# Step i+1's h on TensorE between step i's attention and its y, in a kernel of attention and two MoE layers

## The chip, the cores and the metric

The kernel runs on one core of a Trainium2 chip. The metric is the device time of one execution in microseconds; times of several runs are given by their median.

## The reference

Three layers in fp32. Retention-like attention on q, k, v of shape (4, 8, 576, 64); a dense MoE with 2304 tokens, 512 model and 2048 inner columns; a second MoE in which each of eight experts takes its 288 tokens in order of their gate values.

```python
scores = scale * np.matmul(q, k.transpose(0, 1, 3, 2))
ret = scores * Dmat[None]                  # decay gamma**(i-j), 0 above the diagonal
x = np.matmul(ret, v)                      # -> (2304, 512)
h = x @ w_in                               # first MoE
g = h * np.tanh(np.log1p(np.exp(h)))       # (h > 20: h itself)
x = g @ w_out
logits = x @ w_gate                        # second MoE: greedy assignment, 288 tokens each
for e in range(8):
    out[mask_e] = np.maximum(x[mask_e] @ w1[e], 0) @ w2[e]
```

## The kernel before

fp32 operands are split into a high part and a rest (names ending in h and l), and each product is made of three matmul passes: high by high, rest by high, high by rest.

The attention and the first MoE run together, in one hand-written order (`first_part`). The tokens are cut into nine blocks of 256 (block n), the inner columns into 16 tiles of 128 (tile f). A **step** is one pair (n, f); there are 144. `plan` (line 65) mixes the steps of blocks 0, 1 and 2 in the first 48 steps, because the weights of each tile f are converted while they run; from step 48 on step i is block i // 16, tile i % 16.

A step's work, by function:

- `ff_h` (L309, matmuls at L317): 12 matmuls of TensorE make h (128 inner columns x 256 tokens) in PSUM. Two consecutive steps share a bank: an even step takes a new tile of one of the two tags ph0 and ph1, an odd step writes its second half.
- `ff_a1` (L321): ScalarE makes tanh (L326), square (L327) and a copy with scale (L328) into d; VectorE multiplies two halves (L334).
- `ff_a2`, `ff_b1`, `ff_b2`, `ff_b3`: VectorE's reciprocal (L339), the products with it (L344 on VectorE, or L346 and L347 on GpSimd), VectorE's product with h itself (L352), which reads the PSUM tile a last time, and the split into gh (ScalarE, L358) and gl (L359, on VectorE while weights are converted and on GpSimd later). In iteration i, b2 belongs to step i-1 and b3 to step i-2.
- `ff_y` (L397, matmuls at L411, for the last block `ff_y_last`, L439 and L447): six (or twelve half-sized) matmuls add g @ w_out of step i-3 into the block's two PSUM banks. After a block's last tile, ScalarE and VectorE copy y out (L420, L421).

Between these stand pieces that `slots` assigns to steps. An attention chunk (up to 128 tokens of a batch) has scores (L219 on TensorE, then pm on VectorE, L224), an output (L243, L248, then ScalarE's copy xh at L254 and VectorE's xl at L255) and a state (L273; then ScalarE, L285, for chunks 2 to 7, else VectorE, L281). The logit pieces of p_logits transpose y (L381; copies at L385 on ScalarE and L383 on VectorE) and multiply (L391). Pieces of the `idle` list (a grid for the later search, L630 to L643; logits on VectorE, L368) are taken near the end of an iteration.

Weights are converted by VectorE (L163, L168), ScalarE (L156, L159, L174) and GpSimd (L177), one part per iteration in nearly all of the first 30 iterations.

Each engine works through its own instructions in the order in which the loop emits them; semaphores follow from the tiles that instructions read and write, and PSUM is tracked by bank. The chunk outputs fall into steps 1, 3, 5, 6, 9, 40, 46, 57, 62, 67, 73, 82, 86, 91, 99, 105, 115 and 121; the logit pieces that turn y with ScalarE's copy into steps 48, 51, 56 and 131.

After the steps, `second_part` routes the tokens and runs the eight experts.

Of the kernel before, what the change touches and what calls it, by code (L numbers as in the profile page):

```python
# [64 lines left out]
def plan():  # L65


    spread = lambda a, b, n: [a + (b - a) * k // (n - 1) for k in range(n)]
    own = {i: (0, f) for f, i in enumerate([0, 1, 2, 3] + spread(6, ENDS[0], NF - 4))}
    free = [i for i in range(3 * NF) if i not in own]  # L70
    lead = [i for i in free if i < BEGIN2]
    rest = [i for i in free if BEGIN2 <= i]
    near = [i for i in rest if i <= ENDS[1]]
    ones = lead + [near[k] for k in spread(1, len(near) - 1, NF - len(lead))]
    own.update({i: (1, f) for f, i in enumerate(ones)})
    own.update({i: (2, f) for f, i in enumerate(i for i in free if i not in ones)})
    steps = [own[i] for i in range(3 * NF)]
    steps += [(n, f) for n in range(3, NB) for f in range(NF)]
    return steps


def first_part(ctx, tc, att, att_ht, att_hn, dtab, qtab, ktab, stab, wi, wo, wgb, ydram, L, constants, cst, begin, grid):
# [16 lines left out]
    steps = plan()  # L99
# [42 lines left out]
    class convert:  # L142
# [18 lines left out]
        def x(self):  # L161
            w0 = self.w0
            nc.vector.scalar_tensor_tensor(w0, self.w1, 0x80000000, w0, op0=ALU.bitwise_and,  # L163
                                           op1=ALU.bitwise_or)
# [16 lines left out]
    def x_block(n):  # L181
        if n not in xT:
            if n == 2:
                xT[n] = [sp.tile([P, KT, TB], F32R, tag="x2", name=f"x{k}2", bufs=2) for k in "hl"]
            else:
                xT[n] = [work.tile([P, KT, TB], F32R, tag="x" + k, name="x" + k, bufs=2) for k in "hl"]
        return xT[n]
# [121 lines left out]
    def ff_h(n, f, i):  # L309
        xh, xl = x_block(n)  # L310
        if i % 2 == 0:
            hbank[0] = psum.tile([P, 2, TB], F32, tag=("ph0", "ph1")[i // 2 % 2], name="ph")
        ph = hbank[0][:, i % 2, :]
        k = 0
        for kt in range(KT):
            for w, x in ((winh, xh), (winl, xh), (winh, xl)):
                nc.tensor.matmul(ph, w[f][:, kt, :], x[:, kt, :], start=(k == 0), stop=(k == 11))  # L317
                k += 1
        q2[n, f] = ph

    def ff_a1(n, f, i, alone):  # L321

        ph = q2[n, f]
        d = work.tile([P, 2, P], F32, tag="d", name="d", bufs=2)
        df = d.rearrange("p a b -> p (a b)")
        nc.scalar.activation(df, ph, AF.Tanh, scale=0.5)  # L326
        nc.scalar.activation(df, df, AF.Square, bias=half_b, scale=-0.5)  # L327
        nc.scalar.activation(df, df, AF.Copy, bias=0.5, scale=0.5)  # L328
        u = work.tile([P, 2, P], F32, tag="u", name="u", bufs=3)
        r = u[:, 0, :]  # L330
        if alone:

            r = work.tile([P, DM], BF, tag="scr", name="r").bitcast(F32)[:, :P]
        nc.vector.tensor_mul(r, d[:, 0, :], d[:, 1, :])  # L334
        inv[n, f] = (d, u, r, alone)

    def ff_a2(n, f):
        r = inv[n, f][2]
        nc.vector.reciprocal(r, r)  # L339

    def ff_b1(n, f, eng):
        d, u, r, alone = inv.pop((n, f))
        if alone:
            eng.tensor_mul(u, d[:, ::-1, :], r[:, None, :].to_broadcast([P, 2, P]))  # L344
        else:
            eng.tensor_mul(u[:, 1, :], d[:, 0, :], r)  # L346
            eng.tensor_mul(u[:, 0, :], d[:, 1, :], r)  # L347
        gt[n, f] = u.rearrange("p a b -> p (a b)")

    def ff_b2(n, f):  # L350
        g = gt[n, f]
        nc.vector.scalar_tensor_tensor(g, g, -1.0, q2.pop((n, f)), op0=ALU.add, op1=ALU.mult)  # L352

    def ff_b3(n, f, eng):
        g = gt[n, f]
        gh = work.tile([P, TB], F32R, tag="gh", name="gh", bufs=3)
        gl = work.tile([P, TB], F32R, tag="gl", name="gl", bufs=3)
        nc.scalar.activation(gh, g, AF.Copy)  # L358
        eng.tensor_sub(gl, g, gh.bitcast(F32))  # L359
        gt[n, f] = (gh, gl)  # L360
# [169 lines left out]
        x()  # L530
    for i in range(len(steps) + YL):
        new = i < len(steps)
        if i == 20:
            constants()
        if i == 62:
            stage.__exit__(None, None, None)
            late = tc.tile_pool(name="late", bufs=1)
            WG = late.__enter__().tile([P, E, DM], F32, name="WG")
            nc.sync.dma_start(WG, wgb)
        if now:  # L540
            now.x()
            now.a()
        if old:
            old.l()
        if new:
            n, f = steps[i]
            ff_h(n, f, i)
            for x in slots.get(i, []):
                x()
            ff_a1(n, f, i, bool(now or old))  # L550
        if new:

            eng = nc.vector if now or old else nc.gpsimd
            if i > 1:
                ff_b3(*steps[i - 2], eng)
            ff_a2(n, f)
            if i:
                ff_b2(*steps[i - 1])
            ff_b1(n, f, nc.vector if i == len(steps) - 1 else eng)
        if i == len(steps) - 1:  # L560
            ff_b2(n, f)
            ff_b3(*steps[i - 1], nc.gpsimd)
            ff_b3(n, f, nc.vector)
        if now:
            now.h()
        old, now = now, None
        if nxt and i in CONV:
            now, nxt = nxt, convert() if done[0] < len(parts) else None
            now.x1()
            now.c()  # L570
        for k in range(2 if i % 4 == 0 or TAIL <= i < POP2 else 1):
            if idle:
                idle.pop(0)()
        if late and i > TAIL + BEGIN and not idle:
            late = late.__exit__(None, None, None)
            soon.extend(begin())
        if i >= YL:
            ff_y(*steps[i - YL], i)
# [840 lines left out]
def build(tc, ap, out):  # L1419
    nc = tc.nc  # L1420
    with ExitStack() as ctx:
        pp = ctx.enter_context(tc.tile_pool(name="pp", bufs=1))
        dp = ctx.enter_context(tc.tile_pool(name="dp", bufs=1, space=bass.MemoryType.DRAM))
        cp = ctx.enter_context(tc.tile_pool(name="cp", bufs=1))
        ctx.enter_context(tc.manual_schedule())
        L = pp.tile([P, NT, E], F32, name="L")
        ydram = dp.tile([N, DM], F32, name="ydram")
        cst = {}
        start = []
        cs = ExitStack()  # L1430

        def begin():
            start.append(Search(cs, tc, L, cst))
            return start[0].early()

        with ExitStack() as c1:
            first_part(c1, tc, ap["att"], ap["att_ht"], ap["att_hn"], ap["dtab"], ap["qtab"],
                       ap["ktab"], ap["stab"], ap["wi"], ap["wo"], ap["wgb"], ydram, L, lambda: constants(cp, tc, ap, cst), cst, begin, lambda *a: Grid(cs, tc, L, cst).pieces(*a))
        keep = ctx.enter_context(tc.tile_pool(name="keep", bufs=1, reuse_waits="tile"))
        L0 = keep.tile([P, NT, E], F32, name="L0")  # L1440
        nc.gpsimd.tensor_copy(L0, L)
        with ExitStack() as c2:
            flag = second_part(c2, tc, L, ydram, ap["wx"], cst, out, start[0], True, L0)
            again = nc.values_load(flag[0:1, 0:1], min_val=0, max_val=1)
        cs.close()
        with tc.If(again != 0):
            with ExitStack() as c3:
                general_constants(c3, tc, ap, cst)
                second_part(c3, tc, L0, ydram, ap["wx"], cst, out, Start(c3, tc, L0, cst), False)
# [15 lines left out]
def constants(cp, tc, ap, cst):  # L1465
    nc = tc.nc
    load_constants(cp, tc, ap, cst, (("ident", [P, P], F32), ("J", [P, NJ + 1], F32), ("SCL", [P, 3], F32),
                                     ("pri", [P, E], F32), ("tri", [P, P], BF), ("io", [P, 96], BF),
                                     ("pcv", [P, NT, 2], BF), ("WGN", [P, KT, E], F32)))
    cst["ones"] = cp.tile([P, P], BF, name="c_ones")  # L1470
    nc.vector.memset(cst["ones"], 1.0)
# [69 lines left out]
```

## Time and profile before

| | us |
|---|---|
| median of 3 runs | 839.11 (837.38 to 840.23) |
| profiled execution | 837.55 |
| its span, first to last instruction | 835.5 |
| TensorE busy | 771.1 (92%) |
| VectorE busy | 546.5 (65%) |
| ScalarE busy | 437.5 (52%) |
| GpSimd busy | 475.3 (57%) |

The steps take the time from about 18 to about 536 us. The engine names in rows are PE (TensorE), DVE (VectorE), ACT (ScalarE) and POOL (GpSimd). A matmul's end is modelled, so neighbouring matmuls seem to overlap; starts are the safer numbers.

### The profile page before, as it was taken

What the parts mean: (1) busy time and instruction counts of PE and PEld (TensorE: products, weight loads), DVE (VectorE), ACT (ScalarE), POOL (GpSimd) and SP (SyncE); (2) the same over time, 40 slices, a digit from 0 to 9 for tenths busy, and PEclk for the clock granted to TensorE, in tenths of its full rate; (3) what the DMA queues carried; (4) which work ended last, traced back from release to release, by engine and by line L of the source; (5) the groups of instructions that cost most, each with busy time, mean ns of one, the idle gap of its engine ahead of it and who ended that gap; (6) DMA issues with size and microseconds to landing.
All of it is one profiled execution on the core that took longest, in us unless ns stands there. A gap on an engine that the chain in (4) does not pass through costs nothing.

```text
span 835.5 us, 16274 instructions
## 1 busy us (share of the span) xinstructions
PE 771.1 (92%) x6151; PEld 702.5 (84%) x6151; DVE 546.5 (65%) x1271; ACT 437.5 (52%) x963; POOL 475.3 (57%) x541
## 2 busy tenths in 40 slices
PE   6688888999999999999999999839999999999993
PEld 5577676888998888888888989839999999999992
DVE  4898999755555788897888875676656653442110
ACT  2678888645544445555455555323535553554520
POOL 2534333455545576666676655314877986977811
PEclk9999999999999999999999999959999999999997
DMA  8536344001212310310110000054566664655311
GB/s 317 192 121 218 133 136 145 2 26 51 102 49 104 114 35 5 101 52 29 51 49 27 2 26 2 26 170 146 153 182 187 195 186 150 200 157 173 119 30 32
DMA packets 27320, 87.63 MB, mean 105 GB/s; under 512 B 4448, under 2 KB 5600, under 8 KB 27104
## 3 DMA queue, kind: packets, MB, share of 16 engines
q1 hardware_dynamic: 24160, 77.06, 28.6%
q0 software_dynamic: 3072, 9.44, 3.5%
q8 instruction: 50, 0.82, 0.4%
q14 instruction: 38, 0.31, 0.1%
HBM read 77.05 MB, written 9.44 MB: 104 GB/s over the span
## 4 chain that ended last, share of the span: by engine, by line
PE 69%; DVE 15%; issue 7%; ACT 3%; POOL 3%; DMA 2%; SPq 0%; DVEq 0%; POOLq 0%; ACTq 0%
PE ph L317 20%; PE hp L1256 9%; PE op L1270 8%; PE b_E L411 8%; PE b_F L411 7%; DVE r L339 3%; DVE raw L163 2%; DVE u L344 2%; PE cnt L971 2%; PE b_A L219 2%; PE b_D L248 1%; DVE hot L867 1%; PE b_E L447 1%; DVE y L168 1%; POOL wxl L810 1%
## 5 line engine op out<-in xcount | busy, mean ns | idle before, releaser
L317 PE MATMUL ph<-xh,winh 128*128 128x256 f32 x576 | 164.6, 286 | 17.5 <-ACT d L326 13.0
L317 PE MATMUL ph<-xl,winh 128*128 128x256 f32 x576 | 161.5, 280 | 0.2 <-DVE xl L255 0.2
L317 PE MATMUL ph<-xh,winl 128*128 128x256 f32 x576 | 161.5, 280 | 0.0
L810 POOL TENSOR_TENSOR wxl<-wraw,wxh 128x1024 fp32r<-128x1024 f32 x60 | 142.3, 2396 | 29.4 <-ACT wxh L808 29.0
L359 POOL TENSOR_TENSOR gl<-u,gh 128x256 fp32r<-128x256 f32 x114 | 85.7, 752 | 89.4 <-ACT gh L358 88.6
L317 PEld LDWEIGHTS ph<-xh,winh 128*128 128x128 f32 x576 | 109.2, 190 | 31.9 <-ACT d L326 17.3
L326 ACT ACTIVATE d<-ph 128x256 f32<-128x256 f32 x144 | 54.7, 380 | 130.5 <-PE ph L317 115.0
L317 PEld LDWEIGHTS ph<-xh,winl 128*128 128x128 f32 x576 | 109.5, 190 | 4.4
L339 DVE RECIPROCAL u<-u 128x128 f32<-128x128 f32 x113 | 107.7, 953 | 3.9
L317 PEld LDWEIGHTS ph<-xl,winh 128*128 128x128 f32 x576 | 109.6, 190 | 0.4 <-DVE xl L255 0.4
L334 DVE TENSOR_TENSOR u<-d 128x128 f32<-128x128 f32 x113 | 44.7, 396 | 63.5 <-ACT d L328 54.9
L346 POOL TENSOR_TENSOR u<-d,u 128x128 f32<-128x128 f32 x112 | 52.4, 468 | 51.9 <-DVE u L339 51.8
L808 ACT ACTIVATE wxh<-wraw 128x1024 fp32r<-128x1024 f32 x64 | 67.4, 1053 | 17.4 <-DMA wraw<-in_wx_dram 17.4
L327 ACT ACTIVATE d<-d,half_b 128x256 f32<-128x256 f32 x144 | 73.5, 510 | 4.7
L347 POOL TENSOR_TENSOR u<-d,u 128x128 f32<-128x128 f32 x112 | 68.2, 609 | 8.8
L328 ACT ACTIVATE d<-d 128x256 f32<-128x256 f32 x144 | 60.2, 418 | 4.6
L358 ACT ACTIVATE gh<-u 128x256 fp32r<-128x256 f32 x144 | 57.9, 402 | 2.1 <-DVE u L352 2.0
L368 DVE SCALAR_TENSOR_TENSOR scr<-y,WG 128x512 bf16<-128x512 f32 x64 | 55.3, 863 | 0.4
L1247 DVE SCALAR_TENSOR_TENSOR htl<-hp,hth 128x288 fp32r<-128x288 f32 x64 | 28.4, 454 | 40.3 <-ACT hth L1259 39.8
L1259 ACT ACTIVATE hth<-hp 128x288 fp32r<-128x288 f32 x64 | 26.1, 409 | 51.4 <-PE hp L1256 50.8
L352 DVE SCALAR_TENSOR_TENSOR u<-u,ph 128x256 f32<-128x256 f32 x144 | 52.5, 364 | 0.3
L1256 PE MATMUL hp<-xth,wxh 128*128 128x288 f32 x256 | 50.1, 309 | 0.9 <-DVE htl L1247 0.9
(271 smaller groups left out, 1892.8 us busy)
## 6 DMA issues: line engine op xcount, KB each, us to landing
wraw<-in_wx_dram SPq DMA_DIRECT2D x64, 512.0 KB, 4.4
att<-in_att_dram SPq DMA_DIRECT2D x32, 512.0 KB, 4.9
raw<-in_wi_dram SPq DMA_DIRECT2D x16, 512.0 KB, 3.5
raw<-in_wo_dram SPq DMA_DIRECT2D x16, 512.0 KB, 3.3
ydram<-y SPq DMA_DIRECT2D x9, 512.0 KB, 2.8
WG<-in_wgb_dram SPq DMA_DIRECT2D x1, 2048.0 KB, 7.9
att<-in_att_ht_dram SPq DMA_DIRECT2D x4, 256.0 KB, 3.5
att<-in_att_hn_dram SPq DMA_DIRECT2D x4, 256.0 KB, 4.2
```

The lines of the kernel that those rows point to most:

```text
L317: nc.tensor.matmul(ph, w[f][:, kt, :], x[:, kt, :], start=(k == 0), stop=(k == 11))
L327: nc.scalar.activation(df, df, AF.Square, bias=half_b, scale=-0.5)
L328: nc.scalar.activation(df, df, AF.Copy, bias=0.5, scale=0.5)
L339: nc.vector.reciprocal(r, r)
L347: eng.tensor_mul(u[:, 0, :], d[:, 1, :], r)
L358: nc.scalar.activation(gh, g, AF.Copy)
L359: eng.tensor_sub(gl, g, gh.bitcast(F32))
L411: nc.tensor.matmul(py[n][t], g[:, t * P:(t + 1) * P], w[f], start=(f == 0 and w is woh and g is gh), stop=(f == NF - 1 and g is gl))
L808: nc.scalar.activation(hi, raw, AF.Copy)
L810: rest = lambda eng: eng.tensor_sub(lo, raw, hi.bitcast(F32))
L1256: nc.tensor.matmul(hp, W[kt][w][:, s], x[:, kt, :], start=(k == 0), stop=(k == 11))
L1270: nc.tensor.matmul(op, W[4 + ft // 2][w][:, s], h[:, ft, :], start=(k == 0), stop=(k == 23))
```

## The change

In iteration i the loop used to emit h of step i first, then the step's pieces, then `ff_a1` of step i. Now h of step 0 is emitted ahead of everything in iteration 0, and each iteration emits its pieces, `ff_a1` of step i and then h of step i+1, whose place is therefore ahead of the iteration's idle pieces and of y of step i-3. Nothing else is touched.

```diff
     for i in range(len(steps) + YL):
         new = i < len(steps)
+        if not i:
+            ff_h(*steps[0], 0)
...
         if new:
             n, f = steps[i]
-            ff_h(n, f, i)
             for x in slots.get(i, []):
                 x()
             ff_a1(n, f, i, bool(now or old))
+            if i + 1 < len(steps):
+                ff_h(*steps[i + 1], i + 1)
```

## Rows read from the trace of the kernel before

**Rows 1.** Busy us (count) by stage: PE, PEld, DVE, ACT, POOL; clock; DMA.
```profile
18.00:50.00 32.00, 20.51 (x185) 18.03 (x186) 26.87 (x40) 21.03 (x52) 13.81 (x11) 0.89 0.51 166
...
100.00:150.00 50.00, 43.55 (x252) 34.07 (x251) 48.54 (x97) 43.49 (x95) 16.63 (x13) 1.00 0.39 131
154.00:490.00 336.00, 336.00 (x2531) 300.49 (x2532) 250.14 (x497) 173.21 (x429) 206.51 (x318) 1.00 0.14 50
```
**Rows 2.** Waits of PE from 50 to 150 us: total, times, longest.
```profile
PE ph L317 <- ACT d L326: 6.3, 9, 0.9
PE ph L317 <- DVE u L352: 2.6, 9, 0.3
```
**Rows 3.** Waits of DVE from 50 to 150 us: total, times, longest.
```profile
DVE r L334 <- ACT d L328: 2.4, 1, 2.4
```
**Rows 4.** Timeline, steps 12 to 14: start, duration, work, idle before and releaser.
```profile
86.02 0.36 ACT L326 ACTIVATE d<-ph 128x256 f32<-128x256 f32 x1
...
86.44 0.38 PE L317 MATMUL ph<-xh,winh 128*128 128x256 f32 x1 [0.74 <-ACT d L326]
...
89.37 0.36 DVE L352 SCALAR_TENSOR_TENSOR u<-u,ph 128x256 f32<-128x256 f32 x1
...
89.78 0.39 PE L317 MATMUL ph<-xh,winh 128*128 128x256 f32 x1 [0.32 <-DVE u L352]
```
**Rows 5.** Timeline, end of the conversions: b2(29), then first matmuls of h(32), y(29), h(33).
```profile
153.53 0.36 DVE L352 SCALAR_TENSOR_TENSOR u<-u,ph 128x256 f32<-128x256 f32 x1
...
153.94 0.39 PE L317 MATMUL ph<-xh,winh 128*128 128x256 f32 x1
...
155.45 0.39 PE L411 MATMUL b_A<-woh,gh 128*128 128x512 f32 x1
...
156.82 0.28 PE L317 MATMUL ph<-xh,winh 128*128 128x256 f32 x1
```
**Rows 6.** Timeline: y(0)'s second bank, and VectorE's work on step 4's scores.
```profile
45.72 0.80 PE L411 MATMUL b_B<-woh,gh 128*128 128x512 f32 x1 [2.56 <-DVE xl L255]
...
50.49 0.42 DVE L224 TENSOR_TENSOR pm<-b_C,dt 64x256 f32<-64x256 f32 x1 [0.84 <-PE b_D L219]
```
**Rows 7.** Timeline: first matmul of y(3), and tanh(6).
```profile
58.87 0.50 PE L411 MATMUL b_A<-woh,gh 128*128 128x512 f32 x1
...
59.27 0.38 ACT L326 ACTIVATE d<-ph 128x256 f32<-128x256 f32 x1
```
**Rows 8.** Timeline, step 40: copy xh, tanh(40), first matmuls of y(37) and h(41).
```profile
182.35 0.60 ACT L254 ACTIVATE xh<-b_B 128x512 fp32r<-128x512 f32 x1 [2.98 <-PE b_B L248]
182.84 0.38 ACT L326 ACTIVATE d<-ph 128x256 f32<-128x256 f32 x1
...
182.23 0.50 PE L411 MATMUL b_E<-woh,gh 128*128 128x512 f32 x1
...
183.73 0.28 PE L317 MATMUL ph<-xh,winh 128*128 128x256 f32 x1
```
**Rows 9.** Timeline: b2(91) and h(94), b2(93) and h(96).
```profile
369.44 0.42 DVE L352 SCALAR_TENSOR_TENSOR u<-u,ph 128x256 f32<-128x256 f32 x1
...
370.52 0.28 PE L317 MATMUL ph<-xh,winh 128*128 128x256 f32 x1
...
375.57 0.36 DVE L352 SCALAR_TENSOR_TENSOR u<-u,ph 128x256 f32<-128x256 f32 x1
...
376.13 0.28 PE L317 MATMUL ph<-xh,winh 128*128 128x256 f32 x1
```
**Rows 10.** Timeline: ScalarE's copy of y before step 131, and the grid piece of step 132.
```profile
489.96 0.58 ACT L420 ACTIVATE y<-b_E 128x512 f32<-128x512 f32 x1
...
495.80 0.27 PE L637 MATMUL b_D<-c_ident,g_mm 128*2 128x128 f32 x1 [0.96 <-DVE g_mm L633]
```
**Rows 11.** Timeline, the drain: waits of y(141).
```profile
531.11 0.39 PE L447 MATMUL b_E<-gh,woh 128*128 128x256 f32 x1 [0.42 <-ACT gh L358]
...
531.91 0.38 PE L447 MATMUL b_E<-gl,woh 128*128 128x256 f32 x1 [0.29 <-POOL gl L359]
```

## The prediction

> I write h(i), y(i), S(i) and tanh(i) for TensorE's product h of step i, its product y of step i, step i's attention and logit pieces, and ScalarE's first pass over h(i).
>
> **What bounds the kernel now.** I first read the busy time of the engines by stage, because a share over the whole span mixes stages with different limits. From 154 to 490 us TensorE's busy time equals the stretch, 336.00 of 336.00, at granted clock 1.00; from 100 to 150 us TensorE has 43.55 of 50 and VectorE 48.54 of 50 [rows 1]. So VectorE sets the pace while the weights of the first MoE are converted (to about 154 us), and TensorE from there almost to the end of the steps. Next come TensorE's waits in the VectorE stretch: 6.3 us in front of h for tanh (9 times) and 2.6 us for VectorE's last pass over an older h (9 times) [rows 2]. They look like what the change is after, but VectorE's own waits there are 2.4 us once [rows 3] and 0.84 us once [rows 6]: it has next to nothing to be given. Last, the single instructions show which waits bind. h(13) starts 0.06 us after tanh(12) ends (86.02 + 0.36, then 86.44), although h(13) goes into the other half of the bank; h(14) starts 0.05 us after VectorE has read h(11) (89.37 + 0.36, then 89.78), the last reader of the bank that h(14) takes over [rows 4]. So an odd step's h waits for the tanh of the step before, and an even step's h(m) for VectorE's read of h(m-3). The change keeps both waits, since h(i+1) still follows tanh(i) in the program.
>
> The Trainium skill, "PSUM — Partial Sum Buffer", section "PSUM bank collisions raise a hardware error", says two engines must not touch one bank in the same partitions at once, even at different columns, and that guarding goes by bank and not by address. By that rule the odd wait stays wherever h is put; were the halves free, the 7.0 us below would fall away. By rows 4 the trace agrees with the rule.
>
> **The change part by part.** It adds and removes no instruction; no DMA and no queue other than TensorE's changes order. TensorE's order was h(i), S(i), y(i-3), h(i+1); it becomes S(i), h(i+1), y(i-3). Seen between two attention pieces, y(i-4), h(i) have changed places. Two things follow: every y runs one h later, and between S(i) and h(i+1) there is no y any more. A y takes 1.37 us (155.45 to 156.82) [rows 5], or 1.50 right behind an attention piece (182.23 to 183.73) [rows 8].
>
> *The start, +0.7 us.* y(0) now stands behind h(4), which must wait for the same xl(3) at which y(0) waited until 45.72 [rows 6]. The part of y(0) that used to run ahead of that wait now runs behind it, so S(4) comes up to 0.5 us later, and VectorE, which already waited 0.84 us for S(4) [rows 6], moves with it. Then h(7) takes the place of y(3), at 58.87, but tanh(6), behind the copy of step 6's attention, ends only at 59.27 + 0.38 [rows 7]: S(7) comes 0.7 to 0.8 us later, and tanh(7) and VectorE behind it. These shifts do not add, since VectorE is one chain: I take 0.7 us, ends 0 and 2.
>
> *The VectorE stretch, +1.4 us.* The waits of rows 2 are set by ScalarE and VectorE, which are held by the conversions, so each h starts when it did. TensorE gains nothing there, but has one y fewer behind it when the stretch ends: h(32) still waits for VectorE's read of h(29) (153.53 + 0.36, then 153.94) [rows 5]. From there on TensorE is never idle, so this y of 1.37 us is added to the end.
>
> *The waits behind attention, +7.0 us.* Where step i is even and S(i) ends in a ScalarE copy, that copy stands ahead of tanh(i), and h(i+1), odd, waits for both. Step 40 shows it: the copy starts at 182.35, tanh(40) runs from 182.84 to 183.22, and y(37), from 182.23 to 183.73, covers that today with 0.51 us to spare [rows 8]. Without it TensorE stands from 182.23 to 183.27: 1.0 us. By the plan in the code such steps are 40, 46, 62, 82 and 86 (attention output) and 48 and 56 (turned logits): 7 x 1.0. Ends: 0.6 (a copy of half the tokens, waits partly spent already) and 1.4 each.
>
> *VectorE's read before an even h, +1.7 us.* S(i) is now one y nearer to h(i+2), so VectorE's chain behind S(i) has 1.4 us less. Step 94 has 370.52 less 369.86 = 0.66 us to spare today, step 96 has 0.20 [rows 9], both in one run of VectorE work that begins behind step 91's attention; 1.4 less leaves a wait of 1.2 us in all. Step 46 (VectorE works off step 44's scores) I price at 0.5. Other even steps either hang on their own h, which moves along, or have 1.4 us and more. Ends 0 and 4, since some ten of them come close to nought.
>
> *Step 131, -0.2 us.* S(131) transposes the y that step 130 finishes, and this y now stands directly ahead of it: TensorE waits for ScalarE's copy (0.58 us, and 0.2 around it), +0.8. Against that h(133) now covers the 0.96 us that TensorE waits for the first grid piece [rows 10]. Ends -1 and +1.
>
> *The drain, -0.7 us.* After the last h, TensorE waits 0.42 and 0.29 us for gh and gl [rows 11]. Now four y stand between h(143) and y(143) instead of three, and these waits go. Ends -0.9 and 0.
>
> The second MoE follows the last y and keeps its own waits: nothing.
>
> **Sum.** 0.7 + 1.4 + 7.0 + 1.7 - 0.2 - 0.7 = +9.9 us. The profiled execution took 837.55 us (span 835.5); it would take 847.5. It lies 1.56 us under the median, 839.11; from the median the forecast is 849.0, 1.2% slower.
>
> **The rivals.**
> *The waits behind attention do not come (842.0).* If ScalarE reached tanh(i) before S(i)'s copy, or halves of a bank were not coupled, the 7.0 us vanish and +2.9 is left; without the 1.7 as well, +1.2 (840.3). For it: TensorE has no wait at all in this stretch today. Against it: rows 4, and ScalarE works in the program's order, copy first [rows 8]. 0.09.
>
> *TensorE's waits in front of y decide (faster, 834.9).* The place is the start and the drain: y(0) waits 2.56 us [rows 6], the grid piece and the last y 0.96 + 0.71 [rows 10, 11]. With one h more ahead of each y all 4.2 us may go: 834.9, if nothing comes in return. It decides if TensorE, not VectorE, paces the first 154 us, and the new waits after 154 us stay under 1.7 us together (with more, less than 2.5 us of the 4.2 are left). Against it: VectorE's 48.54 of 50 [rows 1]. 0.04.
>
> *Each new wait also costs clock (859).* From 18 to 50 us, with y(0)'s 2.56 us among other waits [rows 6], TensorE's mean granted clock is 0.89 [rows 1], so 0.11 x 32 = 3.5 us are lost; if each of the seven new waits lost 1.4 us, two fifths of that, it would be +10 more. Against it: from 100 to 150 us TensorE waits up to 0.9 us every other step, and the clock stays 1.00 [rows 1, 2]. 0.05.
>
> *The order on TensorE does not change (839.1).* Only if the queue were reordered behind the program. 0.01.
>
> **How the numbers follow.** The forecast has 0.81, the rivals 0.09, 0.04, 0.05 and 0.01. The low ends of the likely terms (0, 1.4, 4.2, 0, -1, -0.9) give +3.7, the high ends (2, 1.4, 9.8, 4, 1, 0) +18; not all fall together, so I take 843.0 to 855.0, which reaches to the first rival and leaves out about 0.15. A measurement of this kernel can tell some 0.3% (2.5 us) from no change. Slower by more: nearly all of the forecast, the clock rival and half of the first rival, 0.90; within: 0.07; faster: 0.03.
>
> **What would show it.** Right: in the TensorE-bound stretch new idle time of some 1 us in front of h(41), h(47), h(49), h(57), h(63), h(83) and h(87), released by tanh; waits for VectorE's read near steps 94 and 96; h(32) where it was or up to 1 us later, with y(27) and not y(28) behind TensorE; no wait for gh in the drain. Wrong: TensorE without idle time from 154 to 490 us, which leaves at most the first rival; or the conversions ending several us earlier than at 154 us, which would mean that VectorE was waiting for TensorE and I misread rows 1 and 3.

## The result, and the profile after

The changed kernel takes 850.0 us (median of 4 runs, 849.79 to 851.07), the kernel before, run beside it, 839.34 us (4 runs, 837.38 to 840.23): a ratio of 1.0133, with a 95% interval of 1.0113 to 1.0153. The forecast was 849.0, between 843 and 855.

The profiled execution of after took 849.96 us with a span of 848.2; that of before took 837.55 us (span 835.5). So 12.4 us separate the two profiled executions, and 10.7 us the two medians; where the difference between these may come from is told under the start, further down.

The busy time of the engines by stage in after (stretch, us, then PE, PEld, DVE, ACT and POOL busy with their counts, granted clock, DMA share, GB/s), to be held against [rows 1]:

```profile
18.00:50.00 32.00, 21.89 (x178) 19.42 (x178) 26.87 (x40) 22.51 (x56) 13.67 (x10) 0.84 0.50 166
100.00:150.00 50.00, 41.84 (x250) 33.80 (x250) 48.64 (x97) 43.45 (x94) 16.67 (x13) 1.00 0.39 131
155.00:490.00 335.00, 325.32 (x2453) 284.79 (x2454) 243.68 (x478) 169.25 (x410) 199.33 (x304) 1.00 0.14 50
```

VectorE still has 48.64 of 50 us while the weights are converted, so that stage is paced as it was. From 155 us TensorE, which had no idle time at all, now has 335.00 - 325.32 = 9.68 us of it, at the same clock of 1.00. What ends this idle time, TensorE's waits from 155 to 500 us in after (total, times, longest):

```profile
PE ph L317 <- ACT d L326: 7.3, 8, 1.0
PE ph L317 <- DVE u L352: 2.5, 7, 0.5
```

Of the eight waits for tanh, seven stand in front of h(41), h(47), h(49), h(57), h(63), h(83) and h(87), the steps that the prediction listed. Step 40 in after, to be held against [rows 8] (start, duration, work, idle before and releaser):

```profile
185.86 0.60 ACT L254 ACTIVATE xh<-b_B 128x512 fp32r<-128x512 f32 x1 [4.51 <-PE b_B L248]
186.35 0.38 ACT L326 ACTIVATE d<-ph 128x256 f32<-128x256 f32 x1
...
186.78 0.39 PE L317 MATMUL ph<-xh,winh 128*128 128x256 f32 x1 [0.97 <-ACT d L326]
```

The copy, the tanh behind it, and h(41) 0.05 us after the tanh's end (186.35 + 0.38 = 186.73): the chain of [rows 8], with no y beside it.

The eighth wait for tanh was in no term of the sum. The same view around step 36:

```profile
168.93 0.60 ACT L420 ACTIVATE y<-b_A 128x512 f32<-128x512 f32 x1 [2.16 <-PE b_A L411]
169.42 0.38 ACT L326 ACTIVATE d<-ph 128x256 f32<-128x256 f32 x1
169.85 0.38 PE L317 MATMUL ph<-xh,winh 128*128 128x256 f32 x1 [0.73 <-ACT d L326]
```

Step 36 has no attention output, but the copy of block 0's finished y stands at its tanh's place in ScalarE's queue, and does what an attention copy does. The copies of the other blocks stand ahead of the tanh of an odd step; the next h is then an even one in the other bank, and none waits for them. Of the waits for VectorE's last read, the one in front of h(80) was not forecast either:

```profile
330.31 0.36 DVE L352 SCALAR_TENSOR_TENSOR u<-u,ph 128x256 f32<-128x256 f32 x1
...
330.73 0.39 PE L317 MATMUL ph<-xh,winh 128*128 128x256 f32 x1 [0.45 <-DVE u L352]
```

The stage ends at the first matmul of L461, the gate product of the last block. In after and, in the second fence, in before:

```profile
549.14 0.39 PE L461 MATMUL b_D<-c_WGN,yT 128*128 128x8 f32 x2
```
```profile
536.52 0.28 PE L461 MATMUL b_D<-c_WGN,yT 128*128 128x8 f32 x1
```

That is 12.62 us later. From L461 to the end both take the same time: 848.2 - 549.14 = 299.06 in after, 835.5 - 536.52 = 298.98 in before. All of the loss lies in the steps.

**Where the 12.62 us arise.** The start of each h in after, less that of the same h in before, gives a shift for each step; its growth from one step to the next places the loss. (Growth counts more than the idle time listed, 0.97 for h(41) against a growth of 1.01, because the modelled end of the work before overlaps the start.)

| stretch | growth of the shift, us | forecast |
|---|---|---|
| start of the steps, up to h(11) | 1.12 | 0.7 |
| h(37), behind the copy of block 0's y | 0.89 | 0 |
| the seven steps behind attention or turned logits | 7.05 | 7.0 |
| VectorE's read: h(46) 0.59, h(80) 0.61, h(94) 0.53, h(96) 0.39, h(112) 0.61, h(124) 0.62 | 3.35 | 1.7 |
| steps 131 to 135 | 0.16 | -0.2 |
| h(143) to L461: one more y, no waits | 0.06 | 1.4 - 0.7 |
| sum | 12.63 | 9.9 |

### The profile page after: what moved, and what is told of

It is laid out like the page before. It is cut to its first block, busy times and chain, and to the rows that moved or that the text cites. A ratio compares the mean times of both kernels' runs of the same rounds, so it can differ in the third digit from the quotient of the medians.

```text
span 848.2 us, 16272 instructions
## 1 busy us (share of the span) xinstructions
PE 773.9 (91%) x6151; PEld 700.9 (83%) x6151; DVE 549.8 (65%) x1271; ACT 441.0 (52%) x963; POOL 476.3 (56%) x541
## 4 chain that ended last, share of the span: by engine, by line
PE 63%; DVE 18%; issue 8%; ACT 6%; POOL 3%; DMA 2%; SPq 0%; DVEq 0%; POOLq 0%
PE ph L317 17%; PE hp L1259 9%; PE op L1273 8%; PE b_E L411 6%; PE b_F L411 6%; DVE u L339 2%; DVE r L339 2%; PE cnt L974 2%; DVE raw L163 2%; DVE u L344 2%; DVE u L334 1%; PE b_D L248 1%; PE b_A L219 1%; PE b_E L447 1%; PE b_F L447 1%
## 5 line engine op out<-in xcount | busy, mean ns | idle before, releaser
L317 PE MATMUL ph<-xh,winh 128*128 128x256 f32 x576 | 172.1, 299 | 34.1 <-ACT d L326 26.0
L359 POOL TENSOR_TENSOR gl<-u,gh 128x256 fp32r<-128x256 f32 x114 | 88.7, 778 | 87.6 <-ACT gh L358 87.0
L334 DVE TENSOR_TENSOR u<-d 128x128 f32<-128x128 f32 x113 | 48.8, 432 | 47.1 <-ACT d L328 39.5
L328 ACT ACTIVATE d<-d 128x256 f32<-128x256 f32 x144 | 60.2, 418 | 4.5
```

## The experiments

Two groups of kernels ran, each with the kernel before beside it: 839.57 us (19 runs) beside e1 to e4, 840.25 us (21 runs) beside e5 to e8. All but e7 share one driver, in which a condition says which h are made ahead:

```diff
+            if i not in made:
+                made.add(i)
+                ff_h(n, f, i)
             for x in slots.get(i, []):
                 x()
             ff_a1(n, f, i, bool(now or old))
+            m = i + 1
+            if m < len(steps) and (COND):
+                made.add(m)
+                ff_h(*steps[m], m)
```

COND is True (the change itself) unless another is given. Medians of this kernel mix three things, so the following table, worked out from the profiled execution of each kernel, separates them: the start of h(11), the time from there to L461, and the time from L461 to the end of the span.

| kernel | median us | h(11) at | h(11) to L461, against before | L461 to the end |
|---|---|---|---|---|
| before | 839.34 | 79.01 | 457.51 | 298.98 |
| e7, before once more | 841.15 | 81.14 | +0.08 | 300.97 |
| after | 850.0 | 80.13 | +11.50 | 299.06 |
| e1, tanh first | 843.87 | 80.18 | +5.92 | 299.29 |
| e2, ahead from h(34) on | 850.68 | 82.93 | +10.56 | 297.90 |
| e3, ahead up to h(33) | 840.78 | 80.20 | +1.31 | 299.18 |
| e4, ahead from h(133) on | 835.98 | 81.78 | -2.15 | 298.96 |
| e5, one logit piece, y copy moved | 847.74 | 80.30 | +7.95 | 300.54 |
| e6, a bank for each h | 859.52 | 80.69 | +17.61 | 300.09 |
| e8, e1 and e5 together | 842.54 | 78.81 | +3.17 | 299.91 |

The middle column repeats within 0.1 us in the unchanged kernel, while its start moves by 2.1 us and its end part by 2.0. The middle column is therefore what an edit is judged by where the median leaves doubt.

### e1: tanh ahead of the attention pieces

In even steps tanh(i) alone is emitted ahead of the step's pieces, so that no copy stands in front of it on ScalarE; the rest of `ff_a1` stays.

```diff
+            if i % 2 == 0:
+                ff_t(n, f)          # d tile and tanh only
             for x in slots.get(i, []):
                 x()
```

> The changed kernel, but in even steps ScalarE's tanh(i) is emitted ahead of the step's attention and logit pieces, so that it no longer stands behind their copy. Theory (the copy ahead of tanh on ScalarE holds h(i+1)): the seven waits in front of h(41), h(47), h(49), h(57), h(63), h(83) and h(87), 6.6 us together in the changed kernel's trace, go; h(37)'s 0.7 us and VectorE's waits near steps 46, 80, 94, 112 and 124 stay. 850.0 - 6.6 = 843.4, between 842.5 and 844.5. Rival (an h directly behind an attention piece starts late whatever ScalarE does): 850, and the seven waits stay.

Measured: 843.87 us (6 runs, 842.86 to 844.68), ratio 1.0051 [1.0035 to 1.0068]. TensorE's waits from 155 to 500 us in e1:

```profile
PE ph L317 <- DVE u L358: 3.5, 10, 0.5
PE ph L317 <- ACT d L325: 0.7, 1, 0.7
PE b_A L387 <- ACT y L426: 0.5, 1, 0.5
```

The seven waits for tanh are gone; the one left is h(37)'s, whose copy is none of the step's pieces. (The last row is step 131's transposes, waiting for the copy of y.) In e1, h(41) starts with no wait, and ahead of the copy that it waited for in after:

```profile
185.81 0.39 PE L317 MATMUL ph<-xh,winh 128*128 128x256 f32 x1
...
185.93 0.60 ACT L254 ACTIVATE xh<-b_B 128x512 fp32r<-128x512 f32 x1 [2.89 <-PE b_B L248]
```

The steps are 11.50 - 5.92 = 5.6 us shorter than in after. Step by step the seven places give back 7.2 us, and h(42), h(48) and h(64), right behind three of them, take 1.4 again (0.41, 0.52 and 0.50; idle 0.25, 0.34 and 0.34), since there VectorE's read comes last once the tanh does not. So the place of the copy in ScalarE's queue is the cause of the largest term, and most of it is won back by moving one instruction.

### e2: ahead only from h(34) on

COND is `m >= 34`: the old order as long as VectorE sets the pace, so that TensorE has no y left over when that ends.

> h is made one step ahead only from step 34 on; up to step 33 the order is that of the kernel before. Theory (VectorE paces the conversions, so one step ahead brings nothing there and leaves one more y, 1.4 us, besides a start 1.1 us later): 850.0 - 2.5 = 847.5, between 846.7 and 848.3. Rival A (the y left over is made up later): 849 to 850. Rival B (most of the loss arises in the start): 839 to 842.

Measured: 850.68 us (5 runs, 848.05 to 851.03), ratio 1.0127 [1.0107 to 1.0148]. The expectation was missed by 3 us. In the profiled execution h(11), which this edit does not touch, starts at 82.93, 3.92 us later than in before and 2.80 later than in after:

```profile
82.93 0.39 PE L317 MATMUL ph<-xh,winh 128*128 128x256 f32 x1 [0.26 <-ACT d L326]
```

From there the steps are 0.94 us shorter than in after. The left-over y of 1.37 us is gone, and one new wait has come, where the order changes:

```profile
162.67 0.39 PE L317 MATMUL ph<-xh,winh 128*128 128x256 f32 x1 [0.37 <-DVE u L352]
```

1.37 - 0.37 = 1.0: the term has its forecast size, but the median alone would have told the opposite, since the late start covers it. Of the 3.92 us, 2.76 arise between h(7) and h(11), at a meeting of two instructions that the last section shows. That the other four executions also started late is likely from their times and was not seen.

### e3: ahead only up to h(33)

COND is `m <= 33`: only the start and the left-over y remain of the change.

> h is made one step ahead up to step 33 only; from step 34 on the order is that of the kernel before. Theory: 839.3 + 1.1 + 1.4 = 841.8, between 841.0 and 842.6. Rival A (the y left over costs nothing, as TensorE waits elsewhere): 840.4. Rival B (most of the loss arises here): 848 to 850.

Measured: 840.78 us (12 runs, 839.96 to 841.91), ratio 1.0017 [1.0005 to 1.0030]. That is just under the range expected, and nearer to the rival's 840.4 than to the 841.8 of the theory. In the trace, from 155 to 530 us TensorE waits almost only for the grid piece, as before the change:

```profile
PE b_D L644 <- DVE g_mm L640: 1.0, 1, 1.0
PE ph L317 <- DVE u L352: 0.2, 1, 0.2
```

The end of the steps stands at 539.02, 2.50 us after that of before, made of 1.19 at h(11) and 1.31 behind it:

```profile
539.02 0.28 PE L461 MATMUL b_D<-c_WGN,yT 128*128 128x8 f32 x1
```

So the left-over y costs 1.31 against a forecast of 1.37. That the median shows only 1.2 us for both fits the start column: 1.19 holds against the first profiled execution of before, which started early (e7).

### e4: ahead only from h(133) on

COND is `m >= 133`: of the change only what the last steps gain.

> h is made one step ahead only from step 133 on, behind the last attention and logit transposes. Theory: only the two gains are left, the wait for the grid piece (0.96 us) and those of the drain (0.88 us), less up to 0.5 us of wait for VectorE's read in front of h(134): 837.5 to 838.0. Rival (the gains are taken back by another wait before the routing, VectorE's or ScalarE's): 839.3.

Measured: 835.98 us (8 runs, 834.94 to 838.08), ratio 0.9954 [0.9937 to 0.9972]: faster than both kernels, by 0.5% against before, and 1.5 us under the range expected. The grid piece, which waited 0.96 us in before [rows 10], follows the last matmul of an h with no wait:

```profile
499.00 0.28 PE L317 MATMUL ph<-xl,winh 128*128 128x256 f32 x1
499.12 0.27 PE L644 MATMUL b_D<-c_ident,g_mm 128*2 128x128 f32 x1
```

and TensorE has no wait for gh or gl in the drain [rows 11]. From h(11) to L461 the steps are 2.15 us shorter: 0.8 from h(133) to h(135), behind the grid piece, and 1.35 in the drain (h(143) to L461: 8.82 us in before; 8.88 in e4 with one more y of 1.41 in it), more than the 0.88 us listed there as idle. The median is 3.6 us lower, and the interval reaches from there to -2.35 us. So 2.15 us is what the trace places. The other 1.4 us stay open: in the one profiled execution the start is 2.77 us later than in before and the part behind L461 is the same.

### e5: one logit piece per iteration, and the y copy on VectorE

The change, with one of the `idle` pieces instead of two in every fourth iteration, and with the ScalarE copy of block 0's y moved to VectorE.

```diff
-        for k in range(2 if i % 4 == 0 or TAIL <= i < POP2 else 1):
+        for k in range(2 if TAIL <= i < POP2 else 1):
...
-            nc.scalar.activation(y[:, 0, :], py[n][0], AF.Copy)
+            if n:
+                nc.scalar.activation(y[:, 0, :], py[n][0], AF.Copy)
+            else:
+                nc.vector.tensor_copy(y[:, 0, :], py[n][0])
```

> The changed kernel with two pieces of VectorE's work moved: from step 66 on one logit piece per iteration instead of two in every fourth, and both copies of block 0's y on VectorE, so that ScalarE has none ahead of tanh(36). Theory: the waits for VectorE's read in front of h(80), h(112) and h(124) (0.45 us each, 0.6 with the slower first matmul) go, those of h(94) and h(96) shrink, and so does that of h(37) (0.7 to 0.9): 850.0 - 3 = 847.0, between 846 and 848. The seven waits for tanh stay. Rival (VectorE is late from the attention pieces, not from the pair of logits): the waits at h(80) to h(124) stay, 849.

Measured: 847.74 us (6 runs, 846.72 to 849.73), ratio 1.0099 [1.0081 to 1.0116]. TensorE's waits from 155 to 500 us in e5:

```profile
PE ph L317 <- ACT d L326: 6.6, 7, 1.0
PE ph L317 <- DVE u L352: 1.3, 4, 0.5
```

The waits in front of h(37), h(80), h(96) and h(112) are gone; those of h(46), h(94) and h(124) stay (the fourth of the list is h(32)'s), and so do the seven behind attention. The theory expected h(124)'s to go and h(94)'s to shrink, and missed both. The steps are 11.50 - 7.95 = 3.55 us shorter, of which these four places give 0.89 + 0.62 + 0.44 + 0.61 = 2.56; the rest is in steps of under 0.2 us each. So the pairs of logit pieces, which stand in VectorE's queue ahead of its read of h(m-3), made three of the six VectorE waits. Those of h(94) and h(124) have another cause. Ahead of the reads that they wait for, VectorE itself stands idle, first for the copy xh of the attention output of step 91 or 121 (0.69 and 2.11 us), then for ScalarE's L328 (0.91 and 0.64); here for h(94):

```profile
373.10 0.42 DVE L255 TENSOR_TENSOR xl<-b_D,xh 128x256 fp32r<-128x256 f32 x1 [0.69 <-ACT xh L254]
374.44 0.29 DVE L334 TENSOR_TENSOR u<-d 128x128 f32<-128x128 f32 x1 [0.91 <-ACT d L328]
```

That is what the rival says, VectorE late from the attention pieces. It is at most a part of the cause: behind the output of step 99 VectorE stands idle in the same way (1.26 and 0.65 us), and h(102) has no wait. No run takes it away.

### e6: a bank for each h

The change, and from step 66 on three PSUM banks in turn, one for each h, instead of two banks with two h each; the third is taken from attention.

```diff
-        if i % 2 == 0:
+        if i == 66:
+            att_tags.remove("D")
+        if i >= 66:
+            hbank[0] = psum.tile([P, 2, TB], F32, tag=("D", "ph1", "ph0")[i % 3], name="ph")
+        elif i % 2 == 0:
             hbank[0] = psum.tile([P, 2, TB], F32, tag=("ph0", "ph1")[i // 2 % 2], name="ph")
-        ph = hbank[0][:, i % 2, :]
+        ph = hbank[0][:, 0 if i >= 66 else i % 2, :]
```

> The changed kernel, but from step 66 on each h has a PSUM bank of its own, in turn out of three (attention gives up one of its banks), so that no h shares a bank with the one whose tanh still runs. Theory (h(i+1) waits for tanh(i) because both are in one bank): the waits of h(83) and h(87), 1.7 to 1.8 us together, go, and those of h(41) to h(63) stay: 848.2, unless attention waits for its fewer banks. Rival (h waits for ScalarE's copy for another reason than the shared bank): h(83) and h(87) wait as before, 850.

Measured: 859.52 us (4 runs, 857.66 to 859.62), ratio 1.0235 [1.0217 to 1.0254], 11 us above the expectation. What the experiment was for can still be read. h(83), which waits 0.97 us for tanh in after, starts here with no wait, and ahead of the copy in front of that tanh:

```profile
345.05 0.39 PE L321 MATMUL ph<-xh,winh 128*128 128x256 f32 x1
...
345.17 0.60 ACT L254 ACTIVATE xh<-b_A 128x512 fp32r<-128x512 f32 x1 [5.60 <-PE b_A L248]
```

From 290 to 500 us no h waits for a tanh any more; before 290 us, most of which still has two h to a bank, the six waits are there. TensorE's waits in e6 from 155 to 290, and in the second fence from 290 to 500 us:

```profile
PE ph L321 <- ACT d L330: 5.6, 6, 1.0
PE ph L321 <- DVE u L356: 0.6, 2, 0.4
```
```profile
PE ph L321 <- DVE u L356: 6.3, 14, 0.7
```

So an odd h waits for the tanh because both lie in one bank, as the prediction read from [rows 4]; with a bank of its own it does not. What the program waits on is a semaphore set by bank, so this shows the cause of the wait, and not what the chip would do without it. The Trainium skill, "PSUM — Partial Sum Buffer", section "PSUM bank collisions raise a hardware error", asks for guards by bank and not by address; the traces agree with that as the kernel's rule. The price came from elsewhere: now every h, odd ones too, waits for VectorE's read of h(m-3), and 14 waits stand where after has two tanh waits and five for VectorE. Against after, fifteen h lose 8.9 us by this (up to 0.84 each, by the growth of the shift), and seven that waited in after win 4.3: 4.6 of the 6.1 us by which these steps are longer. The rest lies in steps of under 0.2 us. A wait that is taken away where the next one is close behind it, and is due at more steps, is no gain.

### e7: the kernel before once more

No edit; a second profiled execution of before, and more runs.

> The kernel before once more, unchanged, for the spread of its start. Theory (a chance meeting of VectorE's conversion at L168 with GpSimd's scaling of q at L228 in iteration 7 decides by some ns, and costs 2.2 us or more when it happens): h(11) starts between 79.0 and 83 us from execution to execution, and the time is 837 to 843 us with a ratio of 1.00. Rival (the late starts of the two kernels that keep the old order there came from their edits): h(11) at 79.0 as in the first trace, and times within 1 us of each other.

Measured: 841.15 us (12 runs, 839.11 to 842.56), ratio 1.0010 [0.9998 to 1.0021]. Its h(11):

```profile
81.14 0.39 PE L317 MATMUL ph<-xh,winh 128*128 128x256 f32 x1 [0.23 <-ACT d L326]
```

2.13 us later than in the first execution, from the same program. A late start needs no edit; the table's start column is not to be read as an effect of e2 or e4. The meeting that the theory names is not what makes e7 late: L168 and L228 start together here too, at 65.92, and VectorE's goes through as in the first execution. The 2.13 us arise ahead of it, 1.05 at h(0) and 1.04 more at h(2). It is in e2 and e4 that the meeting goes the other way, and there 2.8 and 2.6 us are lost behind it (last section).

### e8: e1 and e5 together

> The changed kernel with all of it together: tanh(i) ahead of the pieces in even steps, one logit piece per iteration, both copies of block 0's y on VectorE. Theory (the costs add): 843.9 - 3 = 840.9, between 840 and 842; what is then left against the kernel before is the y left over at the end of the conversions (1.4 us) and small waits for VectorE's read, less the gains at the grid piece and the drain. Rival (with the waits for tanh gone, VectorE's reads take their place): 843 to 844.

Measured: 842.54 us (10 runs, 840.87 to 844.35), ratio 1.0026 [1.0011 to 1.0041]. TensorE's waits from 155 to 500 us in e8:

```profile
PE ph L317 <- DVE u L358: 2.1, 6, 0.5
PE b_A L387 <- ACT y L427: 0.5, 1, 0.5
```

Had the two savings simply added, the steps would stand at 11.50 - 5.58 - 3.55 = +2.37; they stand at +3.17. The savings add to within 0.8 us, so the terms of the sum are nearly separate. The median lies 0.5 us above the range expected, with a kernel before that was 0.7 us slower in this group than in the first. Of the six waits for VectorE, those of h(42), h(48) and h(64) are the rival's: they are not in after and came when the waits for tanh went. Even with all waits for tanh and three of VectorE's gone, h one step ahead over all the steps does not reach the kernel before.

## Why the prediction was right, point by point

**What bounds.** Held. VectorE has 48.64 of 50 us in its stretch, and h(32) stands at 155.06, as far behind before's 153.94 as h(11) is. TensorE now waits 12.0 us for tanh from 50 to 150 us (6.3 in [rows 2]), and yet the shift is 1.13 at h(13) and 1.10 at h(36): behind the start these waits cost nothing but the left-over y.

**The seven waits, 7.0.** Held in mechanism, place and size: 7.05. e1 removes all seven by the copy's place, e6 the two behind step 66 by the bank; each alone suffices, so both links of the chain that the prediction drew from [rows 4, 8] are shown.

**The left-over y, 1.4.** Held: 1.31 in e3, 1.0 with its counter-wait in e2.

**VectorE's reads, 1.7.** Mis-sized: 3.35. The step that failed is the list. The prediction named steps 46, 94 and 96 and said that other even steps have 1.4 us and more to spare or move along with their own h. For 46 it said 0.5 and got 0.59; for 94 and 96 1.2 and got 0.92. But h(80), h(112) and h(124), which it put among the others, took 1.84 more. The trace of before shows them as near as the named ones: there h(80) and h(112) have 0.12 us to spare and h(124) 0.83, less than 1.4 and, for the first two, less than the named h(94) and h(96). Here VectorE's read of h(77) and then h(80) in before:

```profile
321.64 0.36 DVE L352 SCALAR_TENSOR_TENSOR u<-u,ph 128x256 f32<-128x256 f32 x1
...
322.13 0.32 PE L317 MATMUL ph<-xh,winh 128*128 128x256 f32 x1
```

For 80, 96 and 112, e5 shows the reason: the two logit pieces of every fourth iteration on VectorE. The slack alone does not price the wait: h(128) has 0.12 us as well, and its shift grows by only 0.12.

**No term at all for h(37), 0.89.** The rule "a ScalarE copy stands ahead of tanh(i)" was right, but was applied to the pieces of `slots` alone. The copies of a finished y (L420) go through the same queue, and block 0's stands ahead of the tanh of an even step. e5 shows it by moving block 0's copy.

**The drain, -0.7, and step 131, -0.2.** The drain gave -1.31 (with 1.37 for the extra y), beyond the forecast's end of -0.9. The idle time listed in before is 0.88, the two waits of [rows 11] and a third of 0.17 for gl; what the rest is made of was not looked for. Steps 131 to 135 gave +0.16: h(132) is late by the 0.46 forecast as 0.8, h(133) wins 1.24 at the grid piece, and 0.94 is lost again at h(134) and h(135), where one wait of 0.46 us for VectorE's read now stands.

**The start, +0.7.** Held in mechanism, somewhat under-sized: against the profiled execution of before it is +1.12. ScalarE's state piece of S(7) starts 1.06 us later than in before, tanh(7) follows it, and VectorE waits 0.89 us for step 7's L328, where it had no wait. In before and, in the second fence, in after:

```profile
62.60 1.83 ACT L285 ACTIVATE sd<-b_F,st 64x64 f32<-64x64 f32 x8
```
```profile
63.66 1.83 ACT L285 ACTIVATE sd<-b_F,st 64x64 f32<-64x64 f32 x8 [0.84 <-PE b_F L273]
...
66.91 0.41 DVE L334 TENSOR_TENSOR r<-d 128x128 f32<-128x128 f32 x1 [0.89 <-ACT d L328]
```

0.22 of the 1.06 was there at tanh(6) already (59.49 against 59.27), so step 7 costs the 0.7 to 0.8 that it was priced at; but the two shifts do add, which the prediction denied.

Against other executions of the old order the sign can turn. Kernels that start in the old order had h(11) at 79.01, 81.14, 81.78 and 82.93, those in the new order at 78.81 to 80.69 (six executions, two of them, e1 and e8, with tanh moved as well). The means are 81.2 and 80.05, so by these the new order is 1.2 us earlier; four and six executions do not settle that. It would account for medians that lie 10.7 us apart where the traces differ by 12.4, but the interval of the ratio, 9.5 to 12.8 us, holds both.

That the forecast of 9.9 comes so near the 10.7 is partly luck. Against the traces from which its terms were read, +12.6, it is 2.7 short: 2.3 in the steps (9.2 against 11.5) and 0.4 at the start. But it was added to the median, and the profiled execution of before lay 1.8 us under its median, that of after on its own.

**The rivals.** *The waits do not come*: fell with the seven waits. *The order does not change*: fell with the traces. *TensorE's waits in front of y decide*: its mechanism at the end of the steps is real (e4, 2.15 us), its condition (less than 1.7 us of new waits) was not met. *Each wait costs clock*: fell where it was priced, since from 155 to 490 us the granted clock is 1.00 with all the new waits in it; only from 18 to 50 us is it lower, 0.84 against 0.89 in [rows 1], and the unchanged kernel has 0.82 there in e7, so this is not put down to the change:

```profile
18.00:50.00 32.00, 22.13 (x200) 19.80 (x197) 25.24 (x38) 21.92 (x53) 14.72 (x11) 0.82 0.51 166
```

## What to carry to other kernels

To issue an engine's next work earlier helps only where that engine waits and nothing else paces it; elsewhere, as here behind attention, it can take away the work that covered another engine's delay. Here the same edit costs 11.5 us over all the steps and gains 2.15 us when kept to the last eleven (e4, 0.46% faster by its median), so look for the stretch before choosing the order of the whole loop. When a wait on an engine's queue is priced, list everything that goes into that queue in the iteration, not only the pieces of the plan, and take the slack of every step from the trace rather than of the ones that look likely. Profile the unchanged kernel twice: here its start moved by 2.1 us, more than the start term that was to be measured.

## What the runs showed of the hardware

In the four executions that start in the old order (before, e7, e2 and e4) h(11) varies by 3.9 us, and one meeting of two instructions makes a large part of it. VectorE's L168 and GpSimd's L228 start within 0.02 us of each other in all four. In before's first execution and, in the second fence, in e7 VectorE's goes through:

```profile
63.82 0.69 DVE L168 SCALAR_TENSOR_TENSOR y<-y,raw 128x512 uint32<-128x512 uint32 x1
63.82 1.83 POOL L228 TENSOR_TENSOR att<-att,qt 128x512 f32<-128x512 f32 x1 [0.99 <-PE b_D L219]
```
```profile
65.92 1.83 POOL L228 TENSOR_TENSOR att<-att,qt 128x512 f32<-128x512 f32 x1 [0.99 <-PE b_D L219]
65.92 0.69 DVE L168 SCALAR_TENSOR_TENSOR y<-y,raw 128x512 uint32<-128x512 uint32 x1
```

In e4 GpSimd's goes through, and in e2 in the same way:

```profile
63.96 1.27 POOL L228 TENSOR_TENSOR att<-att,qt 128x512 f32<-128x512 f32 x1 [0.98 <-PE b_D L219]
63.97 1.80 DVE L168 SCALAR_TENSOR_TENSOR y<-y,raw 128x512 uint32<-128x512 uint32 x1
```

VectorE's instruction takes 1.11 us more and GpSimd's 0.56 less. Behind it VectorE is held once more in e4: L359 takes 1.51 us, with GpSimd's L177 beside it, where it takes 0.41 in before. In the stretch where VectorE sets the pace this delays everything that follows: from h(7) to h(11) e4 loses 2.62 us and e2 2.76 against before, e7 0.03. In the new order the two stand apart: in after L168 starts at 64.06 and L228 at 64.87, and in all six kernels that start in the new order VectorE's is ahead by 0.23 us or more and takes 0.69.

The Trainium skill, "SBUF — State Buffer", section "Who interferes with whom", says that a VectorE instruction with two inputs in SBUF contends with a GpSimd instruction that reads SBUF, that the port pair which the two share is an exclusive lock, and that the order of issue decides who blocks. These traces agree in direction: one of the two takes its own time and the other is lengthened, to 1.80 us where 1.27 + 0.69 would be 1.96. Which of the two issued first, starts as close as these do not tell.

The rest of the spread stays open: e7 is 1.05 us late at h(0) and 1.04 more at h(2), e2 1.26 between h(1) and h(2). So do the 297.9 to 301.0 us that the part behind L461 takes.
